# A gated recurrence and a two-layer feed-forward on one core: some loads moved to a second DMA queue, and new tables for the order of the work

## The chip, the core and the metric

The kernel runs on one core of one Trainium2 chip. A core has a matrix engine (TensorE, PE in the profile; its weight loads are PEld), a vector engine (VectorE, DVE), a scalar engine (ScalarE, ACT), a general engine (GpSimd, POOL) and a sync engine (SyncE, SP) that here only issues DMAs. Each engine runs its own instructions strictly in order and waits on semaphores for the others. The metric is the device time of one execution in microseconds; lower is better.

## The reference

For 4 batches, 8 heads, 768 time steps and head size 48, a state per head decays and is read at every step; the result, 3072 tokens of 384 features, goes through a feed-forward with a squared ReLU.

```python
# r, k, v, w: [4, 8, 768, 48]   u: [8, 48]
for t in range(S):
    kt, vt, rt, wt = k[:, :, t], v[:, :, t], r[:, :, t], w[:, :, t]
    cur = einsum('bhd,bhe->bhde', u[None] * kt, vt)
    y[:, :, t] = einsum('bhd,bhde->bhe', rt, state + cur)
    state = wt[:, :, :, None] * state + einsum('bhd,bhe->bhde', kt, vt)
x = y.transpose(0, 2, 1, 3).reshape(4 * 768, 384)
h = maximum(x @ w_in, 0)          # w_in:  [384, 2048]
out = h * h @ w_out               # w_out: [2048, 384]
```

All is fp32. k, v and r are small random numbers, w lies between 0.8 and 0.95.

## The kernel before

**Attention.** Time is cut into 6 chunks of 128 steps; a unit is one chunk c of one batch b. Within a unit DVE scans the decays w along time (line 411), ACT takes their logarithm and the exponential of minus it, so the inverse (418, 419), DVE multiplies the running products into r (422) and their inverse into k (428, 429, 431). PE forms the scores (459); the diagonal comes from u*k*r, which GpSimd multiplies in two steps (438, 440) and DVE sums over the head into `beta` (441), ACT spreads it over a diagonal matrix (448), and DVE copies the scores beside it under a causal mask (463). PE multiplies with v (493) and, from chunk 1 on, with the state (484). ACT and DVE split the result into a high and a low part `x` (525, 526) for the feed-forward. In chunk 0 the tiles w, k and r are transposed by PE (399) straight from the loaded tile; from chunk 1 on DVE transposes 32x32 blocks (367) and 16 small DMAs spread them (377, `pt<-st`).

**Weights.** `w_in` and `w_out` come in 8 groups of two blocks each (`ri` and `ro` are the raw tiles, `wi` and `wo` the split ones). Each tile is split once into a high and a low part by ACT (318), DVE (322, 326, 331), ACT (338) and GpSimd (339), through two scratch tiles `q`.

**Feed-forward.** For a chunk's 512 tokens and each of 16 blocks f of the hidden size, PE makes `hp` with 9 matmuls (573; two PSUM banks take turns), ACT and DVE square and split it into `g` (578, 579, 581, 582; three buffers take turns), and PE adds it into four output banks `ob` with 3 matmuls per batch (588). In chunk 0 the first 6 blocks, and in chunk 1 all 16, are done in halves of two batches (256 tokens) as soon as those batches are ready (`HALF`).

**The order.** No instruction is placed by hand. Each step is given to a planner (class `Plan`) with its engine, a cost, its data and a rank. The planner keeps a model time for every engine; again and again it takes the step that could start soonest, and of those that could start together the one of lowest rank. So the ranks, from tables of offsets by kind of step (`AT`, `AT0` for chunk 0, `WL` and `W0` for weights, `OFF` and `LAG` for the feed-forward), shift which steps go first. The order that comes out is fixed at build time: on the chip every engine runs its list in order, and a step that has to wait holds all behind it. DMA issues are such steps too: on SP's list for nearly all of them, on ACT's for u and the last four outputs. The planner models each queue's wire apart from the other's (`wire`), and lets a DMA issued by ACT take time on ACT.

The functions that the change touches, and what calls them:

Of the kernel before, what the change touches and what calls it, by code (L numbers as in the profile page):

```python
# [169 lines left out]

@with_exitstack
def kernel(
    ctx: ExitStack,
# [37 lines left out]
    wi_r, wi_t, wo_r, wo_t = [], [], [], []  # L213
# [10 lines left out]
    for i in range(3):  # L224
        g = place(f"g{i}", [128, 2, 512], F32R, None)
# [11 lines left out]
    far = const.tile([128, NC * B], F32, name="far")  # L237
# [17 lines left out]
    P = Plan()  # L255
# [42 lines left out]
    def load_w(g, rank):  # L298
        before = first_use(0) if g == NG - 1 else [s for s in P.steps if any(x.pool == "ly" for x in s.slots)] if g == NG - 2 else []

        pairs = w_in32[g, 0:KT * R].rearrange("(k p) x -> p k x", k=KT)
        for j in range(2):
            last = w_in32[g, KT * R + j * D:KT * R + j * D + D].rearrange("(k p) x -> p k x", k=KT)
            for i, (to, n, src) in enumerate(((j * J, D, pairs[j * D:j * D + D]), (j * J + D, J - D, last))):
                P.add("sp", 1.4 if n == D else 0.5, rank, lambda to=to, n=n, src=src: nc.sync.dma_start(out=wi_r[g][to:to + n], in_=src),
                      w=[("wi", g, j, i)], after=before if g == NG - 1 else [], runs=3 * n)
        P.add("sp", 2.4, rank, lambda: nc.sync.dma_start(out=wo_r[g], in_=w_out32[g]), w=[("wo", g, 0, 0)],
              after=before, runs=256)

    def split_w(g, rank):  # L310
# [34 lines left out]
    def attention(c, b, rank):  # L345
        ss = slice(c * C, c * C + C)
        n = (c * B + b) // 2
        pt = pts[n % 2][:, b % 2]
        PT = [("pt", n % 2, b % 2, i) for i in range(3)]
        raw = [("raw", n, q, x, tb) for q, x in ((0, 0), (1, 0), (1, 16), (2, 0)) for tb in range(4)]  # L350
        if b % 2 == 0:
            st = Slot("st" if c else "st0", n)
            both[n] = d = {"st": st}
            after = [both[n - 1]["z"]] if n > 2 else []
            for b0, m in ((b, 1), (b + 1, 1)) if (c, b) == (0, 0) else ((b, 2),):
                for i, src in ((0, w), (2, k), (1, r)):
                    def load(i=i, src=src, b0=b0, m=m):
                        nc.sync.dma_start(out=st.tile.rearrange("s (t b h d) -> s t (b h) d", t=3, b=2, h=H)[:, i, (b0 - b) * H:(b0 - b + m) * H, 0:D],
                                          in_=src[b0:b0 + m, :, ss, :].rearrange("b h s d -> s (b h) d"))
                    P.add("sp", 1.05 * m, rank("load") + b0 - b, load, w=[(st, x, i) for x in range(b0 - b, b0 - b + m)], after=after, runs=128 * H * m)  # L360
# [237 lines left out]
    AT = {"load": -12.5, "z": -10, "pt": -10.5, "rk": -7.0, "beta": -5.0, "far": 9.25, "v": -6.0, "scan": -2.25, "ln": 7.0, "rt": -6, "kn": 3.25, "diag": -3.5, "mt": 5, "mask": 3.25, "ktp": 5.25, "kt": 12.5, "mix": 4.25, "x": 1.5, "x3": -5.0, "send": 3.0, "dS": 3.5, "S": 1.25}  # L598
    AT0 = {"load": -13.0, "turn": -1.5, "rk": -2, "beta": 0.2, "far": 9.25, "v": -6.75, "scan": -1.75, "ln": 5.25, "rt": 0.25, "kn": 2, "diag": 9.5, "mt": -1.0, "mask": 3.75, "ktp": 7.25, "kt": -1, "mix": 3, "x": 7.75, "x3": -1, "send": 4.0, "dS": 7.5, "S": -4}
    U0 = (-16, -15.25, -6.75, -5.5)  # L600
    C1 = (5.25, 13, 34.5, 36)
    WL = (-8.25, -8, -9, -5.5, -1.75, -7, -8.25, -13.5)
    OFF = {"hp": -1.0, "g": -6.5, "ob": 0.75, "os": -7.5}
    W0 = (-12.5, -9.5, -1, 0.25, 0.25, 5.5, 5.0, 17)
    HALF = (6, 16, 0, 0, 0, 0)
    LAG = 2

    def rank_of(c, b):
        if c == 0:
            return lambda nm: U0[b] + AT0[nm]  # L610
        return lambda nm: (C1[b] if c == 1 else 8 * ((c - 1) * B + b) - 4) + AT[nm]

    for b in range(B):
        attention(0, b, rank_of(0, b))
    for g in range(NG):
        load_w(g, W0[g] + WL[g])
        split_w(g, W0[g])
    x = 0
    for c in range(NC):
        if c:  # L620
            for b in range(B):
                attention(c, b, rank_of(c, b))

        order = [(f, bs) for bs in ((0, 2), (2, B)) for f in range(HALF[c])] + [(f, (0, B)) for f in range(HALF[c], NF)]
        for f, bs in order:
            step = (bs[1] - bs[0]) / 2
            ffn(P, c, f, lambda nm, x=x, step=step: x + OFF[nm] + (LAG * step if nm in ("ob", "os") else 0), bs)
            x += step
    with tc.manual_schedule():
        P.run()  # L630
# [101 lines left out]
```

## Time and profile before

| | us |
|---|---|
| median of 3 runs | 559.23 |
| lowest and highest | 558.83, 562.87 |
| profiled execution, its span | 559.9 |
| PE busy | 530.8 (95%) |
| weight loads busy | 466.7 (83%) |
| DVE busy | 359.1 (64%) |
| ACT busy | 288.0 (51%) |
| POOL busy | 101.3 (18%) |

The profiled execution has no time of its own beside its span, so the span is set against the runs. In the groups and waits of the profile, `out<-in` names the tiles that an instruction writes and reads, with buffer numbers left out; `hp<-x,wi` is the first feed-forward product, `ob<-wo,g` the second. "Idle before" is the time the engine stood still just ahead of an instruction, and what ended it. An engine named with q (SPq, ACTq) is its sequencer, which issues DMAs.

### The profile page before, as it was taken

Reading aid. Unit: us, or ns where it says so; the run is one execution under the profiler, and the core shown is the slowest. Engines: PE = TensorE matmul, PEld = TensorE weight load, DVE = VectorE, ACT = ScalarE, POOL = GpSimd, SP = SyncE. Lnnn points to the kernel's source line nnn. Section 1 sums busy time; section 2 is a strip of 40 time slices with the busy share of each in tenths; the row PEclk is TensorE's granted clock in tenths of the full one; section 3 lists DMA queues with packets and bytes.
Section 4 is the critical chain, followed back from the end, with each engine's and each line's share of the span. In section 5 each row is a group of like instructions: output and inputs, shape, how many; then the busy total and the mean of one; then the engine's idle time right before and its main releaser. Section 6 shows DMA issues by size and latency. Waiting matters only on the chain. (4 is left out here: it accounts for less than half of the span.)

```text
span 559.9 us, 10076 instructions
## 1 busy us (share of the span) xinstructions
PE 530.8 (95%) x3800; PEld 466.7 (83%) x3800; DVE 359.1 (64%) x643; ACT 288.0 (51%) x677; POOL 101.3 (18%) x115
## 2 busy tenths in 40 slices
PE   4768898999999999999999999999999999999995
PEld 3557787889998999988888888888888888998994
DVE  5789879898759596776866767567475233332330
ACT  2786776668554747555554554553563222332322
POOL 4253552352203003030401102102000000000000
PEclk9998898999999999999999999999999999999999
DMA  9999699237472645637470470460440000010001
GB/s 156 210 240 217 122 255 218 39 64 137 99 141 51 111 109 91 123 78 135 80 132 2 78 168 24 84 129 2 78 106 3 12 1 1 14 58 2 0 1 60
DMA packets 206326, 50.86 MB, mean 91 GB/s; under 512 B 196032, under 2 KB 201152, under 8 KB 206272
## 3 DMA queue, kind: packets, MB, share of 16 engines
q1 hardware_dynamic: 205552, 49.17, 43.9%
q10 hardware_dynamic: 720, 0.98, 0.5%
q8 instruction: 32, 0.52, 0.4%
q14 instruction: 22, 0.18, 0.1%
HBM read 31.65 MB, written 4.72 MB: 65 GB/s over the span
## 5 line engine op out<-in xcount | busy, mean ns | idle before, releaser
L573 PE MATMUL hp<-x,wi 128*128 128x512 f32 (+1 forms) x1062 | 225.6, 358 | 4.7 <-DVE g L582 4.7
L588 PE MATMUL ob<-wo,g 128*128 128x384 f32 x1152 | 224.7, 341 | 4.4 <-ACT g L581 4.4
L588 PEld LDWEIGHTS ob<-wo,g 128*128 128x128 f32 x1152 | 200.5, 189 | 12.2 <-ACT g L581 4.9
L573 PEld LDWEIGHTS hp<-x,wi 128*128 128x128 f32 x1062 | 175.5, 190 | 31.9 <-DVE g L582 5.8
L579 DVE SCALAR_TENSOR_TENSOR hp<-hp,t 128x512 f32<-128x512 f32 (+1 forms) x118 | 70.2, 596 | 110.5 <-ACT t L578 110.0
L578 ACT ACTIVATE t<-hp 128x512 f32<-128x512 f32 (+1 forms) x118 | 60.9, 516 | 136.8 <-PE hp L573 111.2
L582 DVE TENSOR_TENSOR g<-hp,g 128x512 fp32r<-128x512 f32 (+1 forms) x118 | 69.1, 586 | 37.7 <-ACT g L581 35.9
L581 ACT CAST g<-hp 128x512 fp32r<-128x512 f32 (+1 forms) x118 | 59.2, 504 | 54.6 <-DVE hp L579 54.4
L448 ACT ACTIVATE m<-ident,beta 128x128 f32<-128x128 f32 x192 | 60.5, 395 | 7.0 <-DVE beta L441 7.0
L438 POOL TENSOR_TENSOR st<-st 128x384 f32<-128x384 f32 x24 | 25.1, 1047 | 64.7 <-DVE st L367 63.5
L463 DVE COPY_PREDICATED m<-caus,a 128x512 f32<-128x512 uint8 x48 | 33.0, 731 | 5.5 <-PE a L459 5.5
L459 PEld LDWEIGHTS a<-pt 48*128 48x128 f32 x384 | 25.8, 199 | 11.4 <-issue 7.1
L459 PE MATMUL a<-pt 48*128 48x128 f32 x384 | 30.8, 298 | 4.4 <-DVE pt L431 4.4
L526 DVE SCALAR_TENSOR_TENSOR x<-a,x 112x128 fp32r<-112x128 f32 (+2 forms) x44 | 17.9, 432 | 20.5 <-ACT x L525 19.9
L493 PE MATMUL a<-m,v 128*48 128x128 f32 (+1 forms) x384 | 28.5, 291 | 2.3 <-DVE m L463 1.8
L525 ACT ACTIVATE x<-a 112x128 fp32r<-112x128 f32 (+2 forms) x44 | 15.2, 389 | 28.8 <-PE a L493 28.5
L411 DVE TENSOR_TENSOR_SCAN pt<-pt,zero 112x128 f32<-112x128 f32 x80 | 28.9, 410 | 0.3 <-DMA x<-x 0.3
L493 PEld LDWEIGHTS a<-m,v 128*48 128x48 f32 (+1 forms) x384 | 21.4, 134 | 7.5 <-issue 4.5
L440 POOL TENSOR_TENSOR st<-st,un 128x384 f32<-128x384 f32 x24 | 26.9, 1120 | 1.6
L367 DVE STREAM_TRANSPOSE st<-st 128x1152 f32<-128x1152 f32 x20 | 26.8, 1359 | 0.0
L553 POOL TENSOR_TENSOR S<-S,Ec 112x192 f32<-112x192 f32 x16 | 8.2, 510 | 102.0 <-DVE S L552 102.0
L418 ACT ACTIVATE m<-pt 112x512 f32<-112x512 f32 x24 | 15.2, 635 | 20.1 <-DVE pt L411 15.7
(72 smaller groups left out, 394.5 us busy)
## 6 DMA issues: line engine op xcount, KB each, us to landing
pt<-st SPq DMA_DIRECT2D x80, 96.0 KB, 2.3
ro<-in_moe_w_out_dram SPq DMA_DIRECT2D x8, 768.0 KB, 9.6
v<-in_v_dram SPq DMA_DIRECT2D x24, 192.0 KB, 3.1
ri<-in_moe_w_in_dram SPq DMA_DIRECT2D x16, 288.0 KB, 9.1
st<-in_w_dram SPq DMA_DIRECT2D x11, 384.0 KB, 4.7
st<-in_k_dram SPq DMA_DIRECT2D x11, 384.0 KB, 5.3
st<-in_r_dram SPq DMA_DIRECT2D x11, 384.0 KB, 5.6
pt<-st SPq DMA_DIRECT2D x80, 48.0 KB, 2.5
```

The source lines that it names most:

```text
L411: lambda p=p: V.tensor_tensor_scan(out=pt[:, 0, p], data0=src(0)[:, p], data1=zero.broadcast_to([HP, C]), initial=1.0, op0=ALU.mult, op1=A ...
L440: P.add("pool", 1.0, rank("rk"), lambda: G.tensor_tensor(out=rk(), in0=rk(), in1=un.rearrange("s (h d) -> s h d", d=D), op=ALU.mult), w=[( ...
L448: A.activation(mv(j)[:, p], ident, AF.Copy, scale=beta.tile[:, 2 * p + j:2 * p + j + 1])
L459: T.matmul(mts[j].tile.rearrange("s (p t) -> s p t", p=NP)[:, p], pt[js, 2, p], pt[js, 1, p], start=True, stop=True)
L463: lambda j=j: V.copy_predicated(out=mv(j), mask=caus.unsqueeze(1).broadcast_to([128, NP, C]), data=mts[j].tile.rearrange("s (p t) -> s p t ...
L493: T.matmul(ybv()[j * J:j * J + n_, p], vt.tile[:, o:o + n_], mv(j)[:, p], start=(c == 0 and p == KT), stop=True, skip_group_check=True)
L573: T.matmul(hp.tile[:, 0:n], wi[f][:, wl, kt], xT[:, kt, xl, xs], start=(m == 0), stop=(m == 3 * KT - 1))
L578: P.add("act", 0.5 if full else 0.28, rank("g"), lambda: A.activation(t(), h(), AF.Relu), r=[hp], w=[(g, 1)])
L579: P.add("dve", 0.61 if full else 0.33, rank("g"), lambda: V.scalar_tensor_tensor(out=h(), in0=h(), scalar=0.0, in1=t(), op0=ALU.max, op1=A ...
L581: P.add("act", 0.53 if full else 0.31, rank("g"), lambda: A.copy(out=hi(), in_=h()), r=[hp], w=[(g, 0)])
L582: P.add("dve", 0.61 if full else 0.33, rank("g"), lambda: V.tensor_tensor(out=lo(), in0=h(), in1=hi().bitcast(F32), op=ALU.subtract), r=[h ...
L588: T.matmul(obs[b][:, 0:DM], g.tile[0][:, gl, o:o + C], wo[f][:, wl], start=(f == 0 and m == 0), stop=(f == NF - 1 and m == 2))
```

## The change

Two things are changed. Of chunk 0, the loads of k and v are issued by ACT and those of w and r stay on SP; all eight `w_out` blocks are issued by ACT. And the order tables are new: they have moved into a class `Ranks`, chunk 1 has a table of its own (`AT1`), and nearly every number differs. Durations, data and arithmetic of the steps are as they were, and the planner is the same.

```diff
+class Ranks:
+    AT = {'load': 38.75, 'z': -1, 'pt': 18, 'rk': -2, 'beta': 49.25, 'far': 75.25, 'v': 6.5, 'scan': 108.25, ...
...
+    OFF = {'hp': -53.5, 'g': -7.5, 'ob': 41.5, 'os': -34}
+    LAG = -4
...
-        P.add("sp", 2.4, rank, lambda: nc.sync.dma_start(out=wo_r[g], in_=w_out32[g]), w=[("wo", g, 0, 0)],
+        P.add("actq", 2.4, rank, lambda: nc.scalar.dma_start(out=wo_r[g], in_=w_out32[g]), w=[("wo", g, 0, 0)],
               after=before, runs=256)
...
-                    def load(i=i, src=src, b0=b0, m=m):
-                        nc.sync.dma_start(out=st.tile.rearrange("s (t b h d) -> s t (b h) d", t=3, b=2, h=H)[:, i, (b0 - b) * H:(b0 - b + m) * H, 0:D],
+                    q_, e = ("actq", nc.scalar) if c == 0 and i == 2 else ("sp", nc.sync)
+
+                    def load(i=i, src=src, b0=b0, m=m, e=e):
+                        e.dma_start(out=st.tile.rearrange("s (t b h d) -> s t (b h) d", t=3, b=2, h=H)[:, i, (b0 - b) * H:(b0 - b + m) * H, 0:D],
                                           in_=src[b0:b0 + m, :, ss, :].rearrange("b h s d -> s (b h) d"))
-                    P.add("sp", 1.05 * m, rank("load") + b0 - b, load, ...
+                    P.add(q_, 1.05 * m, rank("load") + b0 - b, load, ...
...
-        P.add("sp", 1.1, rank("v"), lambda: nc.sync.dma_start(out=vt.tile.rearrange("s (h d) -> s h d", d=D),
+        q_, e = ("actq", nc.scalar) if c == 0 else ("sp", nc.sync)
+        P.add(q_, 1.1, rank("v"), lambda e=e: e.dma_start(out=vt.tile.rearrange("s (h d) -> s h d", d=D),
...
-    OFF = {"hp": -1.0, "g": -6.5, "ob": 0.75, "os": -7.5}
-    LAG = 2
```

What this does to the order, at three places. Line numbers of the changed kernel are 34 to 37 higher from the first function on: 418 is 455, 441 is 478, 573 is 610, 588 is 625.

First the start of ACT's list, before. `st00` is the tile of w, k and r of batches 0 and 1, `pt0` the transposed one.

```order
L283 DMA un_122<-in_u_dram 128x384
L418 ACTIVATE m0_150<-pt0_123 112x512
L419 ACTIVATE m0_150<-m0_150 112x512
L421 COPY pt0_123<-ob1_136 112x4
L418 ACTIVATE m1_151<-pt0_123 112x512
```

The same place after the change; `v0` to `v2` are the v tiles of batches 0 to 2, `ro0` and so on the raw `w_out` blocks.

```order
L317 DMA un_122<-in_u_dram 128x384
L424 DMA v0_147<-in_v_dram 128x8x48
L424 DMA v1_148<-in_v_dram 128x8x48
L424 DMA v2_149<-in_v_dram 128x8x48
L394 DMA st00_131<-in_k_dram 128x8x48 x2
L341 DMA ro0_58<-in_moe_w_out_dram 128x2x768
L341 DMA ro2_66<-in_moe_w_out_dram 128x2x768
L341 DMA ro1_62<-in_moe_w_out_dram 128x2x768
L341 DMA ro3_70<-in_moe_w_out_dram 128x2x768
L458 COPY pt0_123<-ob1_136 112x4
L455 ACTIVATE m0_150<-pt0_123 112x512
```

Nine issues now stand ahead of ACT's first computing step. Two more `w_out` blocks (`ro5`, `ro4`) and then the k load of batches 2 and 3 follow among ACT's next steps, the latter as its 27th row; w and r of these batches stand on SP behind the `w_in` pieces of groups 0, 2 and 1.

Second, DVE's list where batch 2 of chunk 0 enters, before. `st01` is the tile of w, k and r of batches 2 and 3, `q0` and `q1` the scratch tiles of the weight split.

```order
L411 SCALAR_TENSOR_TENSOR pt1_124<-ob2_137,zero_121 112x128
L422 TENSOR_TENSOR pt1_124<-ob3_138,pt1_124 112x4x127
L579 SCALAR_TENSOR_TENSOR hp1_140<-hp1_140,t0_92 128x256
L422 TENSOR_TENSOR pt1_124<-ob3_138,pt1_124 112x4x127
L550 TENSOR_TENSOR S1_126<-a0_141,Ec1_159 112x4x48
L441 TENSOR_REDUCE beta2_164<-st01_132 128x8
L582 TENSOR_TENSOR g0_91<-hp1_140,g0_91 128x256
L322 TENSOR_SCALAR q0_143<-q0_143 128x768
L326 SCALAR_TENSOR_TENSOR q0_143<-ri1_60,q0_143 128x768
```

The same place after the change:

```order
L365 SCALAR_TENSOR_TENSOR q1_144<-ri1_60,q1_144 128x768
L563 SCALAR_TENSOR_TENSOR x0_130<-a1_142,x0_130 128x3x128
L448 SCALAR_TENSOR_TENSOR pt1_124<-ob2_137,zero_121 112x128 x4
L478 TENSOR_REDUCE beta2_164<-st01_132 128x8
L459 TENSOR_TENSOR pt1_124<-ob3_138,pt1_124 112x4x127
L616 SCALAR_TENSOR_TENSOR hp0_139<-hp0_139,t0_92 128x256
L616 SCALAR_TENSOR_TENSOR hp1_140<-hp1_140,t1_94 128x256
L619 TENSOR_TENSOR g0_91<-hp0_139,g0_91 128x256
```

The split of weight group 1 (`ri1`) moved ahead of `beta` of batch 2, and the first feed-forward step on DVE (579, now 616) moved behind it.

Third, PE's list in the last chunk, in the steady part of the feed-forward, before:

```order
L573 MATMUL hp1_140<-x1_129,wi3_69 128x512 x9
L588 MATMUL ob0_135<-wo2_67,g2_95 128x384 x3
L588 MATMUL ob1_136<-wo2_67,g2_95 128x384 x3
L588 MATMUL ob2_137<-wo2_67,g2_95 128x384 x3
L588 MATMUL ob3_138<-wo2_67,g2_95 128x384 x3
L573 MATMUL hp0_139<-x1_129,wi3_69 128x512 x9
```

And after the change:

```order
L610 MATMUL hp0_139<-x1_129,wi4_73 128x512 x9
L610 MATMUL hp1_140<-x1_129,wi4_73 128x512 x9
L625 MATMUL ob2_137<-wo2_67,g0_91 128x384 x3
L625 MATMUL ob3_138<-wo2_67,g0_91 128x384 x3
L625 MATMUL ob0_135<-wo3_71,g1_93 128x384 x3
L625 MATMUL ob1_136<-wo3_71,g1_93 128x384 x3
L625 MATMUL ob2_137<-wo3_71,g1_93 128x384 x3
L625 MATMUL ob3_138<-wo3_71,g1_93 128x384 x3
L625 MATMUL ob0_135<-wo3_71,g2_95 128x384 x3
L625 MATMUL ob1_136<-wo3_71,g2_95 128x384 x3
L610 MATMUL hp0_139<-x1_129,wi5_77 128x512 x9
```

One `hp` block and four `ob` steps became two `hp` blocks and eight `ob` steps; such pairs of whole blocks stand 23 times in PE's list, before once.

More of the change, by code (lines that the diff above doesn't have):

```diff
@@ L356, in attention @@
                 for i, src in ((0, w), (2, k), (1, r)):
-                    def load(i=i, src=src, b0=b0, m=m):
-                        nc.sync.dma_start(out=st.tile.rearrange("s (t b h d) -> s t (b h) d", t=3, b=2, h=H)[:, i, (b0 - b) * H:(b0 - b + m) * H, 0:D],
+                    q_, e = ("actq", nc.scalar) if c == 0 and i == 2 else ("sp", nc.sync)
+                    def load(i=i, src=src, b0=b0, m=m, e=e):
+                        e.dma_start(out=st.tile.rearrange("s (t b h d) -> s t (b h) d", t=3, b=2, h=H)[:, i, (b0 - b) * H:(b0 - b + m) * H, 0:D],
                                           in_=src[b0:b0 + m, :, ss, :].rearrange("b h s d -> s (b h) d"))
-                    P.add("sp", 1.05 * m, rank("load") + b0 - b, load, w=[(st, x, i) for x in range(b0 - b, b0 - b + m)], after=after, runs=128 * H * m)
+                    P.add(q_, 1.05 * m, rank("load") + b0 - b, load, w=[(st, x, i) for x in range(b0 - b, b0 - b + m)], after=after, runs=128 * H * m)
             if c > 0:
@@ L595, in ffn @@
                 P.add(q_, 1.1, rank("os"), lambda b=b, os_=os_, ob=ob, e=e: e.dma_start(out=ob[c * C:c * C + C] if s0 is None else ob[ds(s0, C)], in_=os_.tile[:, 0:DM]), r=[os_])
[L598 to L602, printed above, removed]
-    OFF = {"hp": -1.0, "g": -6.5, "ob": 0.75, "os": -7.5}
-    W0 = (-12.5, -9.5, -1, 0.25, 0.25, 5.5, 5.0, 17)
-    HALF = (6, 16, 0, 0, 0, 0)
-    LAG = 2
[L608 to L611, printed above, removed]
     for b in range(B):
-        attention(0, b, rank_of(0, b))
+        attention(0, b, lambda nm, b=b: RANKS.unit(0, b, nm))
     for g in range(NG):
-        load_w(g, W0[g] + WL[g])
-        split_w(g, W0[g])
+        load_w(g, RANKS.load(g))
+        split_w(g, RANKS.split(g))
     x = 0
@@ L621 @@
             for b in range(B):
-                attention(c, b, rank_of(c, b))
+                attention(c, b, lambda nm, c=c, b=b: RANKS.unit(c, b, nm))
         order = [(f, bs) for bs in ((0, 2), (2, B)) for f in range(HALF[c])] + [(f, (0, B)) for f in range(HALF[c], NF)]
@@ L626 @@
             step = (bs[1] - bs[0]) / 2
-            ffn(P, c, f, lambda nm, x=x, step=step: x + OFF[nm] + (LAG * step if nm in ("ob", "os") else 0), bs)
+            ffn(P, c, f, lambda nm, x=x, step=step: RANKS.ffn(nm, x, step), bs)
             x += step
```

21 lines of the change are left out of this document (added).

## The prediction

> **What bounds the kernel now.** I read the page first: its busy table, then the slices.
>
> ```profile
> span 559.9 us, 10076 instructions
> ...
> PE   4768898999999999999999999999999999999995
> ...
> DMA  9999699237472645637470470460440000010001
> ```
>
> TensorE (PE) is busy in nine tenths or more of every slice from the eleventh on. What is not full is the left end, and there the DMA row is full instead. The windows view sizes both; its columns are the window, its length, busy time of PE, weight load, VectorE (DVE), ScalarE (ACT) and GpSimd (POOL), the granted clock, the DMA share and GB/s.
>
> ```profile
> 0.00:20.00 20.00, 9.83 (x46) 7.15 (x48) 13.70 (x30) 9.77 (x25) 8.14 (x21) 1.00 1.02 184
> 20.00:40.00 20.00, 16.69 (x158) 13.77 (x154) 15.19 (x28) 14.00 (x35) 8.73 (x8) 1.00 1.22 225
> 40.00:60.00 20.00, 15.56 (x124) 13.10 (x124) 17.93 (x28) 12.04 (x28) 8.98 (x6) 0.83 1.01 206
> 60.00:80.00 20.00, 17.32 (x152) 16.41 (x148) 15.58 (x30) 17.49 (x46) 9.57 (x6) 1.00 0.72 171
> 80.00:100.00 20.00, 17.98 (x91) 15.23 (x90) 18.53 (x31) 11.21 (x17) 5.97 (x5) 0.91 1.02 222
> 100.00:559.90 459.90, 453.41 (x3243) 400.99 (x3241) 278.17 (x500) 223.48 (x528) 59.91 (x72) 1.00 0.33 67
> ```
>
> PE idles 22.6 us before 100 us (10.17, 3.31, 4.44, 2.68, 2.02) and 6.5 us after it, all of that at the tail. So a change of order can win at most part of the 22.6 us; whatever delays the first 100 us moves the end by as much, since PE has no gap later to make it up. The waits of PE in those 100 us say whom it waits for:
>
> ```profile
> PE ob L399 <- DMA st<-in_w_dram: 5.9, 1, 5.9
> PE hp L573 <- DVE g L582: 4.7, 3, 2.0
> PE a L459 <- DVE pt L431: 4.4, 3, 2.5
> PE ob L588 <- ACT g L581: 4.4, 1, 4.4
> ```
>
> After the first load it is DVE and ACT throughout. DVE is busy 80.9 of the first 100 us: 28.9 of 40, then 52.0 of 60. DVE does the same instructions after the change, so it is its 19.1 idle us that the new order can shrink or stretch.
>
> **The change, part by part.** First the wires. The transfers of the first 60 us, and what one load of each kind moves:
>
> ```profile
> GB/s 0 83 218 172 171 173 166 196 217 217 223 310 252 163 163 164 178 192 235 201 320 287 192 208 205 339 296 108 162 226 272 159 209 196 350 188 197 196 198 195
> DMA packets 26618, 12.30 MB, mean 205 GB/s; under 512 B 23227, under 2 KB 23355, under 8 KB 26614
> ...
> ro<-in_moe_w_out_dram SPq DMA_DIRECT2D x8, 768.0 KB, 9.6
> v<-in_v_dram SPq DMA_DIRECT2D x24, 192.0 KB, 3.1
> ri<-in_moe_w_in_dram SPq DMA_DIRECT2D x16, 288.0 KB, 9.1
> st<-in_k_dram SPq DMA_DIRECT2D x11, 384.0 KB, 5.3
> ri<-in_moe_w_in_dram SPq DMA_DIRECT2D x16, 96.0 KB, 8.1
> ```
>
> One queue alone keeps the 16 engines at a share of 1.02, 1.22 and 1.01 in the first three windows. The change does not lessen the bytes; it lets two queues ask for them at once. If the engines are the limit, what goes earlier on one queue makes something later on the other. The Trainium skill says the same in "DMA: Bandwidth & Descriptors", section "Issuing engines are not separate DMA queues": such DMAs run on the same 16 engines and interleave, and a second issuer only saves issue time. The shares agree for one queue; no trace so far shows two queues of head loads at once. By that rule the time is the sum made below, 562.7 us; without it, the first rival's 552.
>
> Term 1, ACT held by its own issues. The rows for issuing, and for ACT's first work:
>
> ```profile
> 0.84 0.42 ACTq L283 DMA_DIRECT2D un<-in_u_dram  x1
> 8.45 0.63 ACT L418 ACTIVATE m<-pt 112x512 f32<-112x512 f32 x1 [6.36 <-DVE pt L411]
> ...
> 1.96 2.52 SPq L358 DMA_DIRECT2D st<-in_r_dram  x1
> 12.53 0.43 SPq L307 DMA_DIRECT2D ro<-in_moe_w_out_dram  x1
> 13.51 5.65 SPq L358 DMA_DIRECT2D st<-in_k_dram  x1
> ```
>
> An issue takes 0.42 us when the queue is short and 2.52 or 5.65 us when it is full: the issuing engine stands still. On SP that costs nothing else; on ACT the activations stand behind it. ACT now issues five head loads (v of batches 0, 1, 2, k of 0 and 1) and four w_out blocks ahead of its first copy and logarithm. Nine unhindered issues are 9 x 0.42 = 3.8 us, done long before 8.45: cost nothing, the lower bound. But five head loads overfill a queue whose third had to wait on SP. ACT comes free when the fifth is nearly through: nine head loads of 192 KB on both queues, 1.77 MB, at the 184 GB/s of the first window are 9.6 us, with four issues of 0.43 us 11.3; with the first w_in group (2 x 288 + 2 x 96 = 768 KB, 0.79 MB) sharing the wire 13.9; with two groups 18.2, the upper bound. I take 13, near the middle case: ACT's first work moves from 8.45 to 13, +4.5 us for logarithm, exponential, the key products and the scores of batch 0.
>
> Most of this is repaid. The new order converts both blocks of weight groups 0 and 1 before or among the first batches' last steps, where DVE had 11.1 idle us in the first 40. Its rows around the end of that stage, and GpSimd's two products that feed beta:
>
> ```profile
> 33.34 1.05 POOL L438 TENSOR_TENSOR st<-st 128x384 f32<-128x384 f32 x1
> ...
> 34.48 1.04 POOL L440 TENSOR_TENSOR st<-st,un 128x384 f32<-128x384 f32 x1
> ...
> 35.03 0.68 DVE L422 TENSOR_TENSOR pt<-ob,pt 112x508 f32<-112x508 f32 x1
> 35.62 0.35 DVE L550 TENSOR_TENSOR S<-a,Ec 112x192 f32<-112x192 f32 x1
> ...
> 41.13 0.42 DVE L579 SCALAR_TENSOR_TENSOR hp<-hp,t 128x256 f32<-128x256 f32 x1
> 41.47 0.55 DVE L441 TENSOR_REDUCE beta<-st 128x8 f32<-128x384 f32 x1
> 42.17 0.42 DVE L582 TENSOR_TENSOR g<-hp,g 128x256 fp32r<-128x256 f32 x1 [0.16 <-ACT g L581]
> ...
> 43.91 1.28 DVE L428 TENSOR_TENSOR pt<-pt,m 112x512 f32<-112x512 f32 x2
> 45.12 1.28 DVE L429 SCALAR_TENSOR_TENSOR m<-pt,m 112x512 f32<-112x512 f32 x2
> 46.32 0.68 DVE L431 TENSOR_TENSOR pt<-a,m 112x512 f32<-112x512 f32 x1
> ...
> 47.25 0.68 DVE L431 TENSOR_TENSOR pt<-a,m 112x512 f32<-112x512 f32 x1
> ```
>
> Before, DVE finishes the key products of batch 3 at 47.25 + 0.68 = 47.9 us. At that point of the new order it has done nearly the same work: all of batches 0 and 1, weight groups 0 and 1, the start of the feed-forward. So without a new wait I put it there at 47.9 too, the 4.5 us filled into idle time (bounds: 4.5 later, or 4 sooner if half of the left-over idle goes as well).
>
> Term 2, k of batches 2 and 3. Before, it was issued at 13.51, fifteenth on SP. Now it stands on ACT behind six w_out blocks. Bytes in front of its end: nine head loads 1.77 MB; w_in of groups 0, 2 and 1, which SP issues ahead of w and r of these batches, 2.36 MB; six w_out blocks of 768 KB, 4.72 MB; w, r and k themselves, 3 x 384 KB, 1.18 MB: 10.0 MB. The 225 GB/s of the second window, whose mixture is nearest, make 44.6 us; the mean of 205 makes 49; the best slice of 350 would make 29. I take 44.6. GpSimd needs 2.2 us for its products (33.34 to 35.52), so beta of batch 2 can be reduced at 46.8. From that instruction to the last key product DVE has fourteen, itself among them: two each of L441, L579, L582, L428, L429 and L431, one each of L422 and L550, 7.7 us by their durations; as starts follow 1.20 us after a pair of 1.28, 7.3 us. Unhindered it would start at 47.9 - 7.3 = 40.6; now it starts at 46.8, and the feed-forward halves (the two products of line 616) stand behind it on DVE, PE behind them. Cost +6.2 us; bounds 0 (arrival by 38.4) and +10.6 (49 us).
>
> Term 3, SP and DVE later. SP is rid of eight w_out issues and has all w_in issues ahead of the second chunk's transposed copies. Their rows cost it 0.43 us each and PE waits for none of them: nothing. DVE has 8.0 idle us between 40 and 100 (2.07, 4.42, 1.47). The new order takes hp blocks in pairs, so one's ACT step covers the other's DVE step; some of these waits must go, others appear around the conversions that now stand in fours. I take 3 us saved; bounds 0 and 6.
>
> Term 4, pairs in the steady part. The first part of the feed-forward now runs two hp blocks, then eight ob blocks; before it ran one and four. The chain of one block, from the last pure stretch:
>
> ```profile
> 542.80 2.27 PE L588 MATMUL ob<-wo,g 128*128 128x384 f32 x12
> 543.00 0.60 ACT L578 ACTIVATE t<-hp 128x512 f32<-128x512 f32 x1 [2.24 <-PE hp L573]
> 544.90 2.24 PE L573 MATMUL hp<-x,wi 128*128 128x512 f32 x9
> 544.98 0.69 DVE L582 TENSOR_TENSOR g<-hp,g 128x512 fp32r<-128x512 f32 x1 [0.65 <-ACT g L581]
> ```
>
> Four ob blocks take 2.10 us (542.80 to 544.90), one 0.525. From ACT's start to DVE's end are 2.67 us, and ACT starts 0.20 us after PE leaves hp. In a pair the first block's ACT step must wait for the g buffer, freed two ob blocks on, 1.05 us; six ob blocks (3.15 us) then remain before PE wants the same hp bank, against 0.20 + 2.67 = 2.87 us. It fits with 0.28 us to spare, so 0; I add 0.3 for the odd miss.
>
> Sum: 0 + 6.2 - 3 + 0.3 = +3.5 us on the profiled span of 559.9 us, 563.4. The span lies 0.7 us above the median of the three runs (559.23; they reach 562.87), so **562.7 us** on their scale. Own range: 554 (k in time, 5 us saved: 559.9 - 5 - 0.7) to 571 (k at 49 us, the 4.5 not repaid, 3 saved: 559.9 + 10.6 + 4.5 - 3 - 0.7).
>
> **The rivals.** *Two queues bring more.* Slices of 310 to 350 GB/s stand in the first 60 us where w_out moves, and 163 to 173 where head loads alone move, so the engines are not at one fixed ceiling. At 300 GB/s the 10.0 MB are in at 33 us, beta waits for nothing, ACT is free at 1.77 / 0.3 = 5.9 plus 1.7 us of issues, before 8.45. Then terms 1 and 2 vanish, about 4 us of DVE's early idle time fill up and 3 later: -7, 552 us (546 to 558). Against it: shares at 1.0 already.
>
> *The pairs run dry.* In chunks 1 to 4 attention steps stand between the feed-forward's on DVE and ACT. The margin of 0.28 us decides: one DVE step of 0.68 us in the way makes PE wait 0.40 us. Before, a single hp block had four more ob blocks (2.10 us) of slack, and PE shows no wait there. At 25 pairs with one such step each: +10 on the unchanged start, 569; with the start's cost 572 (566 to 577). For it: an order planned to the last tenth; against it: DVE is 60% busy there, 278.17 of 459.90 us, and PE's lateness gives the others time.
>
> *The loads were hidden anyway.* DVE's work bounds the start in both, and the waits only change their names: 559 us.
>
> **How the numbers follow.** Forecast 0.40, more wire 0.35, dry pairs 0.16, hidden 0.09. One per cent, about what a measurement of this kernel can tell from no change, is 553.6 to 564.8. Faster: 0.28 of the second case and 0.05 of the first's lower edge, 0.33. Slower: the third case and 0.15 of the first, 0.31. Between: 0.36. The likeliest is the forecast, 562.7, by itself 554 to 571; as cases of both signs have weight, the range reaches from 547 to 573, with about 1 in 10 left out at either end.
>
> **What would show it.** Term 1: the start of ACT's first logarithm (13 against 8.45) and ACT issue rows of over 1 us. Term 2: DVE or GpSimd waiting for the k load around 41 to 47 us. The wire: GB/s of the first 60 us, 205 to 225 by the forecast, near 300 by the first rival. Pairs: PE waits on line 619 or 615 after 100 us; none by the forecast. If PE's idle time before 100 us falls below 18 us, the forecast is wrong on the good side; above 32, on the bad.

## The result

| | us |
|---|---|
| before, median of 4 runs (lowest, highest) | 559.05 (558.83, 562.87) |
| after, median of 4 runs (lowest, highest) | 580.75 (578.71, 581.95) |
| ratio, 95% interval | 1.036 (1.032 to 1.040) |
| span of the profiled execution, before and after | 559.9, 579.9 |

The change costs 21.7 us. The forecast was 562.7, its range 547 to 573; the time lies outside. The page after, span and slices of PE and of the DMA engines:

```profile
span 579.9 us, 10036 instructions
...
PE   2336699899999999999999999999999999999995
...
DMA  9999885425365563536444247272302000010001
```

PE is full from the ninth slice on (from the eighth before); the loss lies ahead of that. The windows after (length, busy PE, weight load, DVE, ACT, GpSimd, clock, DMA share, GB/s):

```profile
0.00:20.00 20.00, 5.29 (x20) 3.72 (x20) 3.94 (x12) 1.28 (x1) 5.24 (x18) 1.00 1.10 167
20.00:40.00 20.00, 8.00 (x44) 5.99 (x44) 14.25 (x24) 12.95 (x32) 4.78 (x5) 1.00 1.06 284
40.00:60.00 20.00, 11.79 (x124) 10.02 (x125) 10.71 (x22) 9.43 (x20) 8.63 (x7) 1.00 1.20 203
60.00:80.00 20.00, 15.05 (x96) 13.63 (x96) 18.52 (x30) 13.16 (x34) 8.90 (x8) 0.74 0.96 172
80.00:100.00 20.00, 19.77 (x188) 17.34 (x187) 15.98 (x31) 17.73 (x46) 8.49 (x6) 1.00 0.60 119
100.00:120.00 20.00, 17.24 (x77) 14.67 (x76) 15.61 (x26) 12.16 (x21) 4.35 (x4) 0.91 0.34 64
```

PE idles 14.71 + 12.00 + 8.21 + 4.95 + 0.23 = 40.1 us in the first 100 us (22.6 before) and 2.8 us in the next 20 (none before): 20.3 us more, and the span is 20.0 us longer. DVE does 3.94 us of work in the first 20 us in place of 13.70. ACT's list after shows why. The fourth word is the sequencer (ACTq, issuing DMAs) or ACT itself:

```profile
1.30 4.56 ACTq L424 DMA_DIRECT2D v<-in_v_dram  x3
8.90 1.12 ACTq L394 DMA_DIRECT2D st<-in_k_dram  x2
10.56 9.97 ACTq L341 DMA_DIRECT2D ro<-in_moe_w_out_dram  x4
20.57 0.17 ACT L458 COPY pt<-ob 112x4 f32<-112x4 f32 x1 [18.47 <-DMA ro<-in_moe_w_out_dram]
20.67 0.63 ACT L455 ACTIVATE m<-pt 112x512 f32<-112x512 f32 x1
...
35.92 0.62 ACT L488 ACTIVATE st<-st,nfar 128x384 f32<-128x384 f32 x1 [4.42 <-DMA ro<-in_moe_w_out_dram]
```

Nine loads stand ahead of ACT's first copy, and issuing them lasts to 20.53 us; the four w_out blocks take 9.97 of it. (The three v loads are those of batches 1, 0 and 3: the tile names v0 to v2 count buffers, not batches.) The first logarithm comes at 20.67 against 8.45. ACT is held again for 4.42 us ahead of 35.92. Meanwhile SP issues w_in, and w of batches 2 and 3 only behind twelve such pieces; PE transposes it at 47.35 (SP's list, then PE's, then DVE's, after):

```profile
6.65 27.67 SPq L339 DMA_DIRECT2D ri<-in_moe_w_in_dram  x12
34.36 0.42 SPq L394 DMA_DIRECT2D st<-in_w_dram  x1
...
20.18 1.12 PE L436 MATMUL hp<-ident,st 128*128 128x128 f32 x4 [1.09 <-DMA st<-in_k_dram]
...
47.35 1.12 PE L436 MATMUL ob<-ident,st 128*128 128x128 f32 x4 [8.73 <-DMA st<-in_w_dram]
...
58.05 0.53 DVE L478 TENSOR_REDUCE beta<-st 128x8 f32<-128x384 f32 x1
...
64.66 1.29 DVE L468 TENSOR_TENSOR pt<-a,m 112x512 f32<-112x512 f32 x2 [0.38 <-PE a L436]
```

The end of batch 3's key products, the mark that the prediction used, is at 64.66 + 1.29 = 65.95 us against 47.93: 18.0 of the 20.0 us are lost by then.

The 9.97 us of the four w_out issues have two large parts, as the first, third and fourth of them show:

```profile
10.56 3.67 ACTq L341 DMA_DIRECT2D ro<-in_moe_w_out_dram  x1
...
14.81 0.54 ACTq L341 DMA_DIRECT2D ro<-in_moe_w_out_dram  x1
...
20.15 0.38 ACTq L341 DMA_DIRECT2D ro<-in_moe_w_out_dram  x1
```

The first issue itself lasts 3.67 us. After the third, from 15.35 to 20.15, 4.8 us pass in which ACT issues nothing: a wait. In the list of ACT's instructions after, each load names the semaphore that it waits on; there are eight of them for loads, DMAHW0 to DMAHW7, shared by both queues and taken in turn:

```
5 L424 DMA v_149<-in_v_dram 128x8x48
6 L394 DMA st_131<-in_k_dram 128x8x48 [waits DMAHW1_49]
7 L394 DMA st_131<-in_k_dram 128x8x48 [waits DMAHW2_49]
8 L341 DMA ro_58<-in_moe_w_out_dram 128x2x768 [waits DMAHW4_49]
9 L341 DMA ro_66<-in_moe_w_out_dram 128x2x768 [waits DMAHW6_49]
10 L341 DMA ro_62<-in_moe_w_out_dram 128x2x768 [waits DMAHW0_49]
11 L341 DMA ro_70<-in_moe_w_out_dram 128x2x768 [waits DMAHW2_49]
12 L458 COPY pt_123<-ob_136 112x4 [waits PE_49]
```

So an issue waits until the load that had the same semaphore before, the eighth before it over both queues, has landed. The last of the four (row 11) waits on that of batch 1's k (row 7, DMAHW2 as well). PE uses this k at 20.18, and the fourth issue starts at 20.15. SP is held in the same way: of the 27.67 us for its twelve pieces it waits 13.6 for w_out blocks that ACT issued (from the waits of its queue; in all, times, longest):

```profile
SPq L339 <- DMA ro<-in_moe_w_out_dram: 13.6, 3, 8.3
```

### The profile page after: what moved, and what is told of

Read it like the earlier page. It is cut to its first block, busy times and chain, and to the rows that moved or that the text cites. A ratio compares the mean times of both kernels' runs of the same rounds, so it can differ in the third digit from the quotient of the medians.

```text
span 579.9 us, 10036 instructions
## 1 busy us (share of the span) xinstructions
PE 530.4 (91%) x3800; PEld 467.8 (81%) x3800; DVE 355.5 (61%) x643; ACT 290.7 (50%) x677; POOL 98.9 (17%) x115
## 5 line engine op out<-in xcount | busy, mean ns | idle before, releaser
L610 PE MATMUL hp<-x,wi 128*128 128x512 f32 (+1 forms) x1062 | 221.3, 358 | 3.6 <-DVE g L619 3.6
L625 PEld LDWEIGHTS ob<-wo,g 128*128 128x128 f32 x1152 | 199.7, 189 | 11.4 <-ACT g L618 4.6
L448 DVE TENSOR_TENSOR_SCAN pt<-pt,zero 112x128 f32<-112x128 f32 x80 | 31.6, 430 | 1.7 <-issue 1.7
L563 DVE SCALAR_TENSOR_TENSOR x<-a,x 112x384 fp32r<-112x384 f32 (+2 forms) x44 | 18.4, 433 | 23.0 <-ACT x L562 21.0
L436 PE MATMUL ob<-ident,st 128*128 128x128 f32 x32 | 7.2, 375 | 23.0 <-DMA st<-in_w_dram 9.3
L562 ACT ACTIVATE x<-a 112x384 fp32r<-112x384 f32 (+2 forms) x44 | 16.2, 390 | 20.3 <-PE a L530 19.0
L590 POOL TENSOR_TENSOR S<-S,Ec 112x192 f32<-112x192 f32 x16 | 9.5, 599 | 96.6 <-DVE S L589 73.9
```

Of the source, the lines that this page charges most:

```text
L448: lambda p=p: V.tensor_tensor_scan(out=pt[:, 0, p], data0=src(0)[:, p], data1=zero.broadcast_to([HP, C]), initial=1.0, op0=ALU.mult, op1=A ...
L610: T.matmul(hp.tile[:, 0:n], wi[f][:, wl, kt], xT[:, kt, xl, xs], start=(m == 0), stop=(m == 3 * KT - 1))
L625: T.matmul(obs[b][:, 0:DM], g.tile[0][:, gl, o:o + C], wo[f][:, wl], start=(f == 0 and m == 0), stop=(f == NF - 1 and m == 2))
```

## The experiments

Three theories. **A**: ACT is held by its own issues. **B, D**: loads come in the wrong order, first w of batches 2 and 3 (B), then whatever lies behind too many bytes (D). **C**: the new order of computing is slower by itself. A fourth, that the second queue brings bandwidth, was the prediction's first rival. All times are medians, and ratios are against the kernel before in the same job (560.6 to 561.5 us there; 559.05 in the job of the result).

**The changed kernel's order of work, every load on SP.** The planner still plans for two queues, so every engine computes in the changed order; only the issuing engine differs.

```diff
-        P.add("actq", 2.4, rank, lambda: nc.scalar.dma_start(out=wo_r[g], ...
+        P.add("actq", 2.4, rank, lambda: nc.sync.dma_start(out=wo_r[g], ...
-                    q_, e = ("actq", nc.scalar) if c == 0 and i == 2 else ("sp", nc.sync)
+                    q_, e = ("actq", nc.sync) if c == 0 and i == 2 else ("sp", nc.sync)
```

(and the same for v)

> The changed kernel's plan is kept, so that each engine computes in the same order, but the loads that it put on ACT's queue are issued by SP in their planned places. ACT can't be held any more. Theory A: the first logarithm at about 9 us, and 566 to 570 (580.75 less the 11 us). Theory B: w of batch 2 stays behind 8.85 MB on one queue, 43 us at 205 GB/s, so PE scans it no sooner than about 45 us (48.5 in the changed kernel): 576 to 582.

576.45 us, ratio 1.029 (1.024 to 1.033), at the lower edge of what theory B gave. Its lists of ACT, PE and DVE:

```profile
9.30 0.63 ACT L455 ACTIVATE m<-pt 112x512 f32<-112x512 f32 x1
...
42.27 0.89 ACT L352 ACTIVATE q<-ri 128x768 f32<-128x768 f32 x1 [9.33 <-DMA ri<-in_moe_w_in_dram]
...
44.59 1.11 PE L436 MATMUL ob<-ident,st 128*128 128x128 f32 x4 [9.22 <-DMA st<-in_w_dram]
...
61.40 1.29 DVE L468 TENSOR_TENSOR pt<-a,m 112x512 f32<-112x512 f32 x2 [0.35 <-PE a L436]
```

ACT's first logarithm comes 11.4 us earlier, and only 4.3 us of it reach the end. ACT now stands 9.33 us for a w_in group that it converts, PE 9.22 us for w: the hold was real, but behind it the loads were late. The mark is at 61.40 + 1.29 = 62.69 us. Theory A alone falls.

**Tables or queues alone, planned anew.** The tables with all loads planned for SP; the old tables with the queue change; and the changed kernel with the first chunk's loads ranked 60 earlier.

```diff
 e1: -        q_, e = ("actq", nc.scalar) if c == 0 else ("sp", nc.sync)
     +        q_, e = "sp", nc.sync
 e2: the queue lines of the change on the old tables
 e4: -            return self.U0[b] + self.AT0[name]
     +            return self.U0[b] + self.AT0[name] - (60 if name == "load" else 0)
```

(in e1 the same for k and w_out)

> The new order tables, with all loads back on the SP queue (the order is planned anew for one queue). Theory A, ACT is held by its own issues: with no load on ACT its first logarithm comes back from 20.7 to about 9 us and the time falls to 558 to 566. Theory B, the loads' order: w of batch 2 now stands behind three w_in groups and three w_out blocks, 6.5 MB and 32 us at 205 GB/s, against 27.6 us before and 48.5 in the changed kernel: 562 to 568. Theory C, the tables cost by themselves: 572 or more whatever queue is used.

> The old order tables, with k and v of the first chunk and all w_out blocks on ACT's queue. Theory A: seven DMA issues stand ahead of ACT's first copy, so ACT is held to 14 to 18 us and the time is 566 to 574. Theory B: SP issues w of batch 2 right behind the first w_in group, so no product waits for it: 555 to 560. Theory C: as before, 559.

> The changed kernel with w, r and k of batches 2 and 3 ranked ahead of the weights on both queues; ACT still issues w_out between its first steps. Theory B: PE scans batch 2 at 25 to 30 us in place of 48.5 and the time falls to 563 to 570. Theory A: ACT is held as long as before (first logarithm at 18 to 21 us), and the time stays at 576 to 582. If both hold, 566 to 574.

584.59 (1.043), 609.82 (1.086) and 603.17 us (1.076): the first lies where theory C put it, the others far above every band, and all are inconclusive on the question. A rank only says who goes first in one plan; another cost or queue gives another order of everything, which these numbers weren't set for. In e2 PE stands 19.9 us for an r load alone. The other experiments therefore keep the plan and move single things in the finished list.

**Queues alone, on the kernel before as planned.** The old plan, its order of computing and its places for the loads; first k, v and w_out issued by ACT, then only k and v.

```diff
 both: -                        nc.sync.dma_start(out=st.tile...
       +                        (nc.scalar if c == 0 and i == 2 else nc.sync).dma_start(out=st.tile...
 e10:  -        ... lambda: nc.sync.dma_start(out=wo_r[g], in_=w_out32[g]) ...
       +        ... lambda: nc.scalar.dma_start(out=wo_r[g], in_=w_out32[g]) ...
```

(and v like k in both)

> The kernel before with its plan and the order of every engine's work kept, but k and v of the first chunk and all w_out blocks issued by ACT in their planned places. If a second queue brings bandwidth: 552 to 557. If it only moves the issuing: four head loads stand ahead of ACT's first logarithm, 8.45 becomes 9 to 12, each later issue holds ACT for 0.4 to 2 us, and the time is 559 to 567. If the queues by themselves were the change's main cost, 574 or more.

> The kernel before with its plan kept, and only k and v of the first chunk issued by ACT; w_out stays on SP (against 572.17 with w_out on ACT too). If w_out blocks that ACT issues late hold up SP's transposed copies, which wait for the landing of the eighth load before them: those copies are on time again, DVE's 8.3 us wait for them is gone, and the time is 561 to 567. If the loss comes from ACT's head loads: 570 to 574.

With w_out on ACT 572.17 us, 1.017 (1.014 to 1.021), between the bands given; without it 562.76, 1.003 (1.001 to 1.005), as expected. In the first, the semaphores of three rows of the order (two of SP's transposed copies, then one of ACT's w_out blocks):

```
40 L377 DMA pt_123<-st_146 16x24x32 [waits DMAHW6_49]
41 L377 DMA pt_123<-st_146 16x24x32 [waits DMAHW7_49]
97 L307 DMA ro_82<-in_moe_w_out_dram 128x2x768 [waits DMAHW7_49]
```

And the waits of SP's queue up to 100 us, the rate from 60 to 95 us in 40 slices, ACT's list and DVE's:

```profile
SPq L377 <- DMA ro<-in_moe_w_out_dram: 16.6, 3, 12.4
...
GB/s 346 205 262 91 36 0 84 89 87 155 150 69 75 39 0 0 0 0 0 0 0 0 53 211 414 418 414 315 148 159 357 260 148 81 25 3 139 149 152 82
...
78.82 0.38 ACTq L307 DMA_DIRECT2D ro<-in_moe_w_out_dram  x1
...
94.69 1.69 DVE L411 TENSOR_TENSOR_SCAN pt<-pt,zero 112x128 f32<-112x128 f32 x5 [8.25 <-DMA pt<-st]
```

SP's copies for chunk 1 wait 16.6 us, 12.4 at once, for w_out blocks. The block ro_82 stands in ACT's list behind ACT's work and is issued only at 78.82; a copy has its turn on the same semaphore behind it. Eight slices of 0.875 us, 72.3 to 79.3 us, pass with nothing moved at all: an issue that is late on one queue holds the other, and DVE waits 8.25 us for the copies. With w_out back on SP no copy waits for one, and 9.4 of the 10.9 us are gone. With w_out on ACT the mark is at 52.6 us, 4.7 behind the kernel before; the other 6 of the 10.9 us come after it, where this wait is.

**w, r and k of batches 2 and 3 ahead of all weights,** in the changed kernel with both queues, then with SP alone.

```diff
 def run(self):
-        for s in self.order():
+        todo = self.order()
+        head = [s for s in todo if s in self.early]
+        todo = [s for s in todo if s not in self.early]
+        at = next(i for i, s in enumerate(todo) if s in self.weights) if head else 0
+        for s in todo[:at] + head + todo[at:]:
             s.fn()
```

(`early` are the three loads of batches 2 and 3, `weights` the weight loads)

> The changed kernel, every engine's computing in the same order, with only w and r of batches 2 and 3 moved ahead of the weights on SP and their k ahead of the weights on ACT. Theory B, w of batch 2 is late: PE scans it with no wait for the load, and 568 to 572. Theory D, bytes: what lands in front makes the weight blocks 1.18 MB later, 5.8 us at 205 GB/s, and DVE, which converts them in its fixed order ahead of batch 2, waits for those instead: 576 to 583.

> The same move of w, r and k of batches 2 and 3 where SP issues every load (against the 576.45 us of the plan kept with all loads on SP). Theory B: 566 to 570. Theory D: w_in of the third converted group ends behind 10 MB, at 46 us in place of 42, DVE waits for it: 574 to 581.

585.70 and 583.94 us (1.044, 1.039): worse than the 580.75 and 576.45 that they are to be set against, and above both bands. Theory B, w alone, falls. In the second, ACT stands 10.21 and 11.59 us for weight blocks: 

```profile
28.00 0.89 ACT L359 ACTIVATE q<-ro 128x768 f32<-128x768 f32 x1 [10.21 <-DMA ro<-in_moe_w_out_dram]
...
53.52 0.89 ACT L359 ACTIVATE q<-ri 128x768 f32<-128x768 f32 x1 [11.59 <-DMA ri<-in_moe_w_in_dram]
```

ACT and DVE convert groups 0 and 1 ahead of batch 2 in the changed order, and these bytes now come later.

**The loads sorted, step by step (SP alone, order of computing unchanged).** e11 keeps batches 2 and 3 in front and puts each w_out behind its w_in, in the order 0, 2, 1 in which the tables load w_in. e12 sorts by the order in which ACT converts, 0, 1, with batches 2 and 3 behind group 1. e15 moves w, k, r of the second chunk ahead of group 3; e17 also v behind group 0. e20 sorts the whole stream: 0, 1, 2, 3, 4, 6, 5, 7, the transposed copies behind group 4.

```diff
+        turn = (0, 1, 2, 3, 4, 6, 5, 7)
+        group = lambda s: s.group if s in self.early else turn[next(k for k in s.keys if k[0] in ("wi", "wo"))[1]]
+        queue, sent, due = sorted(spots, key=group), set(), 0
...
```

(the sorted loads are then taken one by one at the loads' planned places)

> As the run before it, and each w_out block issued right behind the w_in group of its own number, in place of six w_out blocks among the first two groups. The third converted group is then complete behind 7.7 MB, 37 us at 205 GB/s. Theory D: DVE's waits for converted weights shrink and the time falls to 562 to 569. If the order of computing is the cost, and the loads only move waits about: 574 or more.

> The changed kernel's order of computing with every load on SP, and the loads in the order in which that order of computing converts the weights: w_in and w_out of group 0, then of group 1, then w, r, k of batches 2 and 3, then the other groups. (The run named loads in order of use had group 2 ahead of group 1, which is converted second.) Theory D, late weight bytes: group 1 is complete behind 4.9 MB, about 26 us, so DVE doesn't wait 8 us for it, scans batch 2 at 34 to 37 us in place of 46, and the time is 562 to 568. Theory C, the order of computing is dear with any order of loads: 574 or more.

> As the run with loads as converted (576.45 us, all on SP), and w, k, r of the second chunk's first pair moved ahead of the weight groups 3, 5 and 7. Before its end lie 8.85 MB in place of 13.6, so it is in at 45 us in place of 74. Theory D: DVE's wait of 15.1 us for it goes, the next to be late is a weight group, and the time is 562 to 569. Theory C, the order of computing is dear by itself: 573 or more.

> As the run before it, and the three v loads of the first chunk, which the changed order of loads has in front, moved behind group 0's weights: w, r, k of batches 0 and 1 come 0.59 MB or 3 us earlier, ACT's first logarithm at 8.4 to 8.8 us (9.66), and 1 to 3 us less than that run: 560 to 567.

> The changed kernel's order of computing, all loads on SP, and the whole stream of loads in the order of use: weight groups 0, 1, 2, 3, 4, 6, 5, 7 as ACT converts them (the tables load w_in of 0, 2, 1, 3, 5, 7, 4, 6), w, r, k of batches 2 and 3 behind group 1, w, k, r of the second chunk behind group 2, its transposed copies behind group 4. Theory D, the order of loads is the loss: DVE's 8.2 us wait near 84 us goes, PE's idle time before 100 us falls to 23 to 28 us, and the time is 560 to 567. Theory C, the order of computing is dear by itself: 572 or more.

577.21, 576.45, 575.14, 579.62 and 567.09 us; ratios 1.029, 1.028, 1.030, 1.037, 1.011 (1.007 to 1.016). The last is at the upper edge of its band. The first four miss theory D's bands, and by their time e11, e12 and e15 fall to theory C; the traces of e12 and e15 tell it otherwise. e11 kept group 2 ahead of group 1, so its name promised too much. e17 meets the late copies of e15 again (DVE waits 7.0 us); why it is 4.5 us above e15 isn't shown. DVE's list of e12, then DVE's and SP's of e15, show where the gains went:

```profile
37.01 0.41 DVE L461 TENSOR_TENSOR_SCAN pt<-ob,zero 112x128 f32<-112x128 f32 x1
...
50.75 1.29 DVE L481 TENSOR_TENSOR pt<-a,m 112x512 f32<-112x512 f32 x2 [0.35 <-PE a L449]
...
74.14 1.38 DVE L416 STREAM_TRANSPOSE st<-st 128x1152 f32<-128x1152 f32 x1 [15.12 <-DMA st<-in_r_dram]
```

```profile
92.85 0.42 DVE L462 TENSOR_TENSOR_SCAN pt<-pt,zero 112x128 f32<-112x128 f32 x1 [8.21 <-DMA v<-in_v_dram]
...
73.04 7.84 SPq L427 DMA_DIRECT2D pt<-st  x9
...
89.59 0.62 SPq L427 DMA_DIRECT2D pt<-st  x1
```

In e12 batch 2 is scanned at 37.01, as expected, and the mark is reached at 52.04 in place of 62.69; then DVE waits 15.12 us for the second chunk's r, which the tables put behind the weights of groups 5 and 7. In e15 that wait is gone and an 8.21 us one follows ahead of 92.85. The row names a v load; by SP's list the transposed copies start at 73.04, behind all w_in groups, and the last is issued at 89.59. In both, the time that the repair won went to the next late transfer. Only with the whole stream sorted do 9.4 us reach the end. Its windows:

```profile
0.00:20.00 20.00, 8.40 (x40) 6.06 (x40) 11.26 (x24) 5.70 (x12) 8.25 (x21) 1.00 1.01 180
20.00:40.00 20.00, 11.72 (x105) 8.94 (x104) 15.33 (x25) 14.46 (x33) 7.68 (x6) 1.00 1.25 216
40.00:60.00 20.00, 14.97 (x122) 13.46 (x122) 18.09 (x34) 16.64 (x42) 9.39 (x8) 0.83 1.03 214
60.00:80.00 20.00, 19.82 (x191) 17.21 (x190) 18.41 (x32) 15.29 (x41) 9.01 (x6) 1.00 0.69 114
80.00:100.00 20.00, 17.52 (x90) 15.20 (x90) 16.12 (x28) 13.52 (x25) 6.24 (x5) 1.00 1.07 243
```

PE idles 27.6 us before 100 us, 5.0 more than in the kernel before. Its largest wait, and DVE's row at the mark:

```profile
PE a L520 <- DVE m L524: 7.4, 1, 7.4
```

```profile
49.15 1.29 DVE L492 TENSOR_TENSOR pt<-a,m 112x512 f32<-112x512 f32 x2 [0.35 <-PE a L460]
```

The mark is at 50.44 us, 2.5 behind the kernel before, in place of 62.69: late loads were most of what was lost by then. Of the span, 564.2 us, 513.8 come after the mark, 1.8 more than before. DVE converts both blocks of group 0 ahead of the masked copies that PE waits for. That this makes part of the 5.6 us that are left is argued, not tried.

**The sorted loads on two queues.** The same three lists of loads (e12, e17, e20), with k, v and w_out on ACT as the change has it.

```diff
-        # e12, e17, e20: nc.sync for k, v and w_out
+        # e13, e18, e21: nc.scalar
```

> The same order of loads with k, v of the first chunk and w_out on ACT's queue, as the change has it. Each load's issue waits for the landing of the eighth load before it, on whichever queue that was. Theory A: two w_out blocks and five head loads still stand ahead of ACT's first work, which starts at 12 to 17 us: 568 to 576, that is 4 to 9 above the run with SP alone. If the order of loads was the whole loss: within 2 us of it.

> As the run before it, with k, v of the first chunk and w_out on ACT's queue, as the change has it. Theory A: the queue change costs by itself, through ACT's held issues and the landing of the eighth load before: 3 to 11 us above the run on SP alone (4.3 with the change's tables, 11 with the old plan). If a second queue brings bandwidth once the loads are in a good order: 2 to 6 us below it.

> As the run before it, with k, v of the first chunk and w_out on ACT's queue, as the change has it. Theory A: ACT's first work waits for the issues in front of it, 13 to 18 us in place of 9.4, and the time is 4 to 11 above the run on SP alone. If a second queue brings bandwidth: 2 to 6 below it.

577.34, 579.86 and 580.12 us: 0.9, 0.2 and 13.0 above their one-queue partners. The first two fell short of what theory A gave (e13 came out as the other theory there had it, within 2 us); the last is a little over it. In e21 ACT's lists show the hold (14.93 and 26.20), against 9.31 for the same copy in e20:

```profile
14.93 0.17 ACT L482 COPY pt<-ob 112x4 f32<-112x4 f32 x1 [12.83 <-DMA st<-in_k_dram]
...
20.28 5.87 ACTq L358 DMA_DIRECT2D ro<-in_moe_w_out_dram  x1
26.20 1.28 ACT L509 ACTIVATE m<-ident,beta 128x128 f32<-128x128 f32 x4 [5.65 <-issue]
```

All pairs side by side, k, v and w_out on SP and on ACT (times in us; the second row's are from two jobs):

| order of computing, order of loads | SP alone | both queues | second queue costs | GB/s of the first 60 us, SP alone and both |
|---|---|---|---|---|
| before's, before's | 561.2 | 572.2 | 10.9 | 205, 192 |
| changed, the tables' | 576.5 | 580.8 | 4.3 | 215, 218 |
| changed, batches 2 and 3 first | 583.9 | 585.7 | 1.8 | 208, 216 |
| changed, as converted | 576.5 | 577.3 | 0.9 | 210, 216 |
| changed, v behind group 0 | 579.6 | 579.9 | 0.2 | 195, 216 |
| changed, all as used | 567.1 | 580.1 | 13.0 | 203, 203 |

The second queue is faster in none. It costs most with the two orders of loads that are fastest on one queue, and little where another late transfer hides the hold: the two losses overlap and don't add. Its bandwidth, in the rows behind the second and the fifth line of the table, SP alone and then both:

```profile
DMA packets 20080, 12.91 MB, mean 215 GB/s; under 512 B 16104, under 2 KB 16232, under 8 KB 20077
```

```profile
DMA packets 21023, 13.07 MB, mean 218 GB/s; under 512 B 17053, under 2 KB 17181, under 8 KB 21020
```

```profile
DMA packets 25122, 11.70 MB, mean 195 GB/s; under 512 B 22094, under 2 KB 22222, under 8 KB 25118
```

```profile
DMA packets 26471, 12.97 MB, mean 216 GB/s; under 512 B 23134, under 2 KB 23262, under 8 KB 26467
```

Two queues move from 13 GB/s less to 21 more, and no time is lower. The 21 stand in a pair whose times differ by 0.2 us; whether a gain there cancels a hold, and why that pair alone moves so much more, isn't shown.

No version beat the kernel before.

## Why the prediction was wrong

**What bounds the kernel** was right: the loss is all in PE's first 120 us and goes to the end undiminished. PE's idle time before 100 us, 40.1, is past the 32 that the prediction named as the bad side.

**Term 1, ACT held, failed, in size and more so in its "repaid".** It put ACT's first work at 13, 18.2 at most; it came at 20.67. The working took a full queue for the cause and let w_out issue in 0.43 us each once the head loads were through. Long issues are there (3.44 us for the last v, 3.67 for the first w_out), but the runs show another wait on top: the landing of the eighth load before, over both queues (4.8 us ahead of the fourth w_out alone). The delay, 12.2 us in place of 4.5, was to be filled into idle time. In e3, without the hold, the mark is at 62.69, 3.3 us sooner, so 3.3 of the 18.0 us come from it and 14.8 stand without it.

**Term 2, late loads, had the right place and the wrong load.** It took k of batches 2 and 3 to land at 44.6. It was issued at 35.50 and its kind took 11.9 us to land, 47.4 us. But w of the same batches was no sooner (PE uses it at 47.35), and behind w stands more: from PE's transpose at 47.35 to the reduction of beta at 58.05 are 10.7 us, where the prediction gave k 2.2 us and put beta at 46.8. Beta needs no w. But PE, held for w, transposes r late, and GpSimd starts its products only behind that, at 53.42; and in DVE's list the scans of w stand ahead of beta, with a wait for another late product of PE between them:

```profile
52.32 0.36 DVE L587 TENSOR_TENSOR S<-a,Ec 112x192 f32<-112x192 f32 x1 [3.39 <-PE a L581]
```

The term counted w and r as bytes ahead of k and never asked who waits for them. It also looked at one load only; the second chunk's loads and the transposed copies, which it left out and term 3 called free, are the next to be late once the first are mended (e12, e15). In the kernel after, DVE waits only 0.4 us for the second chunk's r. The landings of the first 60 us after (issues, size and median us from issue to landing):

```profile
ro<-in_moe_w_out_dram ACTq DMA_DIRECT2D x7, 768.0 KB, 13.3
st<-in_w_dram SPq DMA_DIRECT2D x1, 384.0 KB, 12.9
st<-in_k_dram ACTq DMA_DIRECT2D x1, 384.0 KB, 11.9
```

Terms 1 and 2 together were to cost 6.2 us to the mark; it came 18.0 later: 3.3 go with the hold (e3), 12.2 more with the sorted loads (62.69 to 50.44), and 2.5 are left in e20.

**Term 3, 3 us saved later,** didn't come: from the mark to the end after takes 579.9 - 65.95 = 513.95 us against 511.97, 2.0 more. **Its other half, SP relieved at no cost,** falls with e12 and e15: there DVE's next wait is for what stands behind w_in on SP.

**Term 4, pairs in the steady part,** was right. After 100 us PE waits for the feed-forward's DVE step only at the edge of the start:

```profile
PE hp L610 <- DVE g L619: 3.1, 2, 2.8
```

2.8 of it lie in the window from 100 to 120; 0.3 us are left for all the rest. The pairs don't run dry, and that rival falls.

**The first rival, two queues bring more,** is refuted: none of the six rates on two queues is above 218 GB/s, where it took 300, and none of the six times is lower. The sentence of the Trainium skill, "DMA: Bandwidth & Descriptors", section "Issuing engines are not separate DMA queues", says that a second issuer only saves the time of issuing. The six times agree; the 21 GB/s more of one pair it doesn't explain. Here the time lay in long issues and in waiting to issue, 9.97 us for four blocks, and the move from SP to ACT put both on an engine with work behind it. **Loads hidden anyway** gave 559 us and falls too: the start is bound by them.

**What is settled.** Ratio 1.036 for the change; 1.029 with all loads on SP; 1.011 with the loads sorted as well. So of the 3.6% some 0.7 are the queue's (the two intervals just overlap), 1.7 the order of loads that the tables make, and 1.1 are left, in which the order of computing and what may still be late among the loads aren't separated. The shares hold in this sequence of repairs only: sorting the loads without undoing the queue (e21) gains nothing, 580.1.

## What to carry to other kernels

Before loads are put on a second issuing engine, ask what an issue waits for and what stands behind it on that engine: here the same bytes, at 215 and 218 GB/s, put off ACT's first work by 12 us, and in e10 a block that ACT issued late held SP's copies. Write the stream of loads beside the order of use, in bytes and for every load to the end of the start, not for the first late one; while several loads are late, mending one may only show the next. A table of ranks belongs to the costs and queues that it was set for: with either changed alone it lost 4 to 9%.

## What was not expected of the hardware and its program

Eight semaphores shared by both queues bound what can be under way: a load on either waits for the landing of the eighth before it. The Trainium skill states, in "DMA: Bandwidth & Descriptors", section "Anatomy of one DMA — SWDGE (gpsimd) path", that a semaphore wait for a DMA happens on the issuing sequencer and not in the DMA engines; the trace agrees, ACT standing 4.8 us ahead of its fourth w_out issue. Under this load a block of 768 KB took 13.3 us from issue to landing in the kernel after (9.6 before), so eight are soon used up; and in e10 one block issued late left all 16 DMA engines without work for 7.0 us (the eight slices at 0 GB/s) while SP had copies to issue. Beside that wait an issue itself can be long: 3.67 us for one w_out block on ACT, 7.14 us for r of batches 2 and 3 on SP.
